# A recurrent transformer segment loop: left output products in one segment of a group, or by halves in two

## The chip, the cores and the metric

The kernel runs on one core of a Trainium2 chip. The core has TensorE (PE) for matrix products, VectorE (DVE), ScalarE (ACT) and GpSimd (POOL) for work on elements, SyncE (SP), which here only issues transfers, and 16 DMA engines. SBUF is the on-chip memory of 128 partitions; PE writes its results to PSUM, whose eight banks each hold 512 float32 values per partition. The metric is the device time of one execution in microseconds (us); the time before is the median of three executions.

## What is computed

```python
xn = layernorm(x)                                  # 2048 tokens x 1024
# A: 64 segments of 32 tokens, one after the other
mem = mem0                                         # 8 rows x 1024
for s in range(64):
    h = concat([mem, xn[32 * s:32 * s + 32]])      # 40 rows
    q, k, v = h @ Wq, h @ Wk, h @ Wv               # 32 heads of 128
    p = softmax(where(mask, q @ k.T * 128 ** -0.5, -1e9))
    o = (p @ v) @ Wo                               # 40 rows x 1024
    mem = o[:8]                                    # goes into the next segment
    outs.append(o[8:])
# B: a feed-forward block over all tokens
ff = gelu(xn @ w1 + b1) @ w2 + b2                  # inner width 3584
out = x + concat(outs) + ff
```

The four weight matrices of A hold 32 MB in bf16, and every segment needs all of them, so the segments' weights don't fit on chip. The memory rows make the segments a chain.

## The kernel before

**Stages.** First comes B with the layer norm, to about 440 us; its result plus x lies in DRAM as `R_n`. Then 64 segments run.

**Weights.** Each segment uses 64 weight tiles, called units, of 128 x 2048 (512 KB): 16 each of Q, K, V and O. 47 stay in SBUF. 17 are streamed, of which two are kept in PSUM and copied by DVE (L267) and 15 come by DMA on SP's queue (L278) through a ring of six slots; a slot is given the next streamed unit when PE is done with the one in it (`unit_done`). The order of the units is fixed by `PLACED`.

**Main and left rows.** A PE product with 32 columns of weights-side operand holds 32 rows of h, but a segment has 40. So the kernel takes 32 rows as "main": the first 24 of the segment's own rows (`NX`) and the 8 memory rows. The last 8 rows (`NL`) of four segments are put together into 32 "left" rows of a group (`GRP`), whose q, k and v are made for four segments at once. A segment's place in its group is `i4` = s mod 4. The left rows' products for K, Q and V are spread over the segments (`left_k`, `left_q`, `left_v`), one half (`u`, 16 heads) at a time. Left rows do not feed the memory, so they may be finished later.

**A segment.** `half_pass` makes K, Q and V of each half, `product` with four column tiles of 32 (L769, 512 columns each). Between them stand `scores` (L886, L892), `exps`, `sums` (L924, L930) and `values` (L978, L984), whose results are copied from PSUM by ACT for r = 0 and by DVE for r = 1 (L997). Then come the 16 O units (`O_UNITS`) with `o_product` (L1027); the value products of half 1 stand after unit `VALUES_1` = 5 among them.

**Output products.** In a segment without left output the main rows' products fill the four column tiles so: units 0 to 8 (`NPAIR` = 9) in products of 512 columns, two for each head; then `fold` adds the two halves of the bank together (ACT L1045, DVE L1048) while units 9 to 15 run in products of 256 columns into a new bank; a DVE add (L1163) makes the result. In the segment with left output (`left_o`: i4 = 1, and the last segment) every head has four products of 512 columns, two for the main rows and two for the 32 left rows of four segments, all into one bank `psX`, with no folding. ACT copies the bank (L1159). The memory rows of the result go through `put_mem` (L314, L324) into the next segment's h. Six units of left products of a coming half pass (`lead_products`) are made ahead to fill PE meanwhile.

**Results and small transfers.** The result is added to the segment's rows of `res_d` (L1184; loaded at L1124). A segment without left output stores its 24 rows straight to `out` (L1218, four stores). The one with left output adds its left rows to `resL_d` (loaded into `pd_main` at L1150), writes main and left rows to a DRAM buffer `outL_d` (L1190), and these are later copied DRAM to DRAM to `out` (L1215). Such copies, and the last of the copies from `R_n` into `res_d` and `resL_d` made by `turn_R` (L486), wait in a list `small`, from which `unit_done` issues one or two on POOL's queue. The loads and stores of segments 0 to 4 (`EARLY_SEGS` = 5) are issued by ScalarE, of later ones by GpSimd (`loads`).

**PSUM.** Three banks, `acc0` to `acc2`, are handed out by `new_acc` and given back by `let_go`; one bank, `mixed`, serves the scores, sums and memory rows; four, `kept`, hold the two weight units.

Of the kernel before, what the change touches and what calls it, by code (L numbers as in the profile page):

```python
# [17 lines left out]
P = 128  # L18
# [19 lines left out]
NX = 24  # L38
# [13 lines left out]
EARLY_SEGS = 5  # L52
# [12 lines left out]
AT_BANKS = 4  # L65

# [48 lines left out]
def kernel(  # L115
# [39 lines left out]
    outL_d = dram.tile([NGRP, 2 * SEG, DM], BF16, name="outL_d")  # L155
# [145 lines left out]
    left_outs, left_keys = [t[:, :, 0:SEG] for t in ko], [t[:, :, 2 * NL:] for t in ko]  # L301
# [29 lines left out]
    with tc.tile_pool(name="ma", bufs=2) as ma, tc.tile_pool(name="mps", bufs=6, space=PSUM) as mps:  # L331
# [95 lines left out]
        def keep_xT(tg, xnT):  # L427
            xl = [t[:, 0:512].rearrange("p (g k i t) -> p g k i t", g=2, k=KT, i=GRP) for t in ko_flat]
            for half in range(2):
                nc.sync.dma_start(  # L430
                    out=rows_d[16 * tg:16 * tg + 16, :, 128 * half:128 * half + 128].rearrange("s p c -> p s c"),
                    in_=xnT[half].rearrange("p s k t -> p s (k t)"),
                )
                for g in range(4):
                    nc.gpsimd.tensor_copy(
                        out=xl[g // 2][:, g % 2, 4 * half:4 * half + 4, :, :],
                        in_=xnT[half][:, 4 * g:4 * g + 4, :, NX:SEG].rearrange("p i k t -> p k i t"),
                    )
# [10 lines left out]
        def main_row(slot):  # L449

            return NL * slot + NL

        def with_left(seg):

            return seg % GRP == 1 or seg == NSEG - 1

        def turn_R(ttg, eng, small=None):

            for i in range(4):
# [3 lines left out]
                both = [  # L465
                    t.rearrange("(h r) c -> r h c", h=2)
                    for t in (res_d[min(4 * og + 1, NSEG - 1) + 1, :, :], resL_d[og, :, :])
                ]
                halves = [rows.rearrange("t (h w) c -> t w h c", w=2)[:, w, :, :] for w in range(2)]
                if with_left(seg):  # L470
                    m0 = SEG
                    pairs = [(both[w][m0:m0 + SEG, :, :], halves[w]) for w in range(2)]
                else:
                    pairs = [(res_d[seg + 1, :, :].rearrange("(j t) c -> t j c", j=4), rows)]
                rows_at = [NL * slot]
                if seg < 2:
                    rows_at.append(NL * (slot ^ 2))
                elif seg >= NSEG - 2:
                    rows_at.append(2 * NL + NL * slot)
                for r0 in rows_at:  # L480
                    pairs += [(both[w][r0:r0 + NL, :, :], halves[w][NX:SEG, :, :]) for w in range(2)]
# [192 lines left out]
    with tc.tile_pool(name="late", bufs=1) as late, \  # L674
# [67 lines left out]
        for s in range(NSEG):  # L742
# [15 lines left out]
            left_o = i4 == 1 or final  # L758
            og, slot = divmod(s + 2, GRP)
            m0 = SEG if left_o else main_row(slot)  # L760
# [80 lines left out]
            def turn_kL(ps, u):  # L841
                kL[u] = left_keys[u]
                turn(ps, kL[u], nc.vector.tensor_copy if first else nc.scalar.copy)
# [14 lines left out]
            def q_left(u):  # L858

                if i4 >= 2 + u and more:  # L860
                    q = qS[:, i4 - 2 - u, :, :]
                else:
                    q = qL[u][:, :, NL * i4:NL * i4 + NL]
# [6 lines left out]
            def keep_q(u):  # L870

                n = 2 - u
                copy_bits(
                    mixed[:, 340:340 + 64 * n].bitcast(U32).rearrange("p (i h t) -> p h i t", i=n, h=16),
                    qL[u].bitcast(U32)[:, :, (GRP - n) * NL // 2:].rearrange("p h (i t) -> p h i t", i=n),
# [22 lines left out]
            def exps(u):  # L898

                if u:  # L900
                    prA = q_all[:, 512:672].rearrange("p (c q) -> p c q", q=40)
                    c0 = 24 if i4 == 1 else 16
                    prB = ko[1][:, 0:8, c0:c0 + NL].rearrange("p (c a) q -> p c a q", a=2)
# [8 lines left out]
                for p, m in (  # L912
                    (prA[:, :, NL:SEG], mask_order), (prB, mask_left[:, i4, :].rearrange("p (a q) -> p a q", a=2))
# [5 lines left out]
            def sums(u):  # L919
# [25 lines left out]
                else:  # L945
                    c0 = 0 if first else NL * slot
                    pdB = left_outs[1 if first or i4 >= 2 else 0][:, :, c0:c0 + NL].rearrange(
# [22 lines left out]
            def values(u, rs):  # L970

                V, (pdA, pdB) = st["V", u], st["pd", u]
                av = {r: new_acc() for r in rs}
                oV = {r: av[r][:, 0:320].rearrange("p (c b q) -> p c b q", c=4, b=2) for r in rs}
                for c in range(4):
                    for r in rs:
# [3 lines left out]
                            start=(c == 0), stop=False, skip_group_check=True, tile_position=(64 * r, 0),  # L980
# [8 lines left out]
                for r in rs:  # L989
# [3 lines left out]
                        (left_outs[u][:, h, NL * slot:NL * slot + NL], 0, NL),  # L993
# [4 lines left out]
                    let_go(av[r])  # L998
# [9 lines left out]
            def o_product(n, t, acc):  # L1008
# [4 lines left out]
                for k in range(2):  # L1013
                    h = 4 * (i % 4) + 2 * u + k
                    main = (outM if i >= 4 else nat_home)[:, h, :]
                    if left_o:
                        lhs = [(0, 32, left_outs[i // 4][:, h, :]), (32, 32, main)]
                        tiles = [(64 * r + r0, w, (2 * r, 2 * r + 1), lhsT) for r0, w, lhsT in lhs for r in range(2)]
                        start, stop = n == 0 and k == 0, n == 15 and k == 1
                    elif n < NPAIR:  # L1020
                        tiles = [(64 * k + 32 * r, 32, (r, r + 2), main) for r in range(2)]
                        start, stop = n == 0, n == NPAIR - 1
                    else:
                        tiles = [(32 * r, 32, (r,), main) for r in range(4)]
                        start, stop = n == NPAIR and k == 0, n == 15 and k == 1
                    for r0, rows, blocks, lhsT in tiles:
                        nc.tensor.matmul(  # L1027
                            acc[r0:r0 + rows, 0:256 * len(blocks)],
                            lhsT=lhsT,
# [5 lines left out]
                        )  # L1035

# [82 lines left out]
            if apart:  # L1119
                ahead_v = left_keys[1]  # L1120
# [14 lines left out]
            at = {VALUES_1[i4]: [lambda: values(1, (0, 1))]}  # L1135
            if apart:
                at[VALUES_1[i4] + 1] = [moved_values]
            psX = new_acc()
            for n, unit in enumerate(O_UNITS):
                t = unit_tile(unit)  # L1140
                if n == NPAIR and not left_o:
# [6 lines left out]
                if n == 6 and left_o:  # L1148
                    st["resL"] = pd_main[:, 0:256]
                    loads.dma_start(  # L1150
                        out=st["resL"], in_=resL_d[og, :, :]
                    )
            nw = 2 if left_o else 1
            if not final:
                o_sb = outM
                no = 16 if left_o else 8
                o = psX[:, 0:32 * no].rearrange("p (h e) -> p h e", e=32)
                if left_o:
                    nc.scalar.copy(out=o_sb[:, 0:no, :], in_=o)  # L1159
                else:  # L1160
                    o = psX[:, 0:256].rearrange("p (h e) -> p h e", e=16)
                    flat = o_sb.rearrange("p h e -> p (h e)")[:, 0:256].rearrange("p (h e) -> p h e", e=16)
                    nc.vector.tensor_tensor(out=flat, in0=o, in1=st["folded"], op=ALU.add)  # L1163
                ahead = []
                if (i4 == 3 or more) and not final:
# [7 lines left out]
                put_mem(o_sb, nxt["hT"], mixed[:, 224:288], 4 // nw)  # L1173
# [3 lines left out]
            tiles = (res, st["resL"]) if left_o else (res,)  # L1177
            for w, r in reversed(list(enumerate(tiles))):
                if left_o:
                    o = psX[:, 256 * w:256 * w + 256].rearrange("p (h e) -> p h e", e=32)  # L1180
                else:
                    o = o_sb[:, 0:8, :]
                r_rows = r.rearrange("p (h e) -> p h e", e=32)
                nc.vector.tensor_tensor(out=r_rows, in0=o, in1=r_rows, op=ALU.add)  # L1184
                if left_o and not final:

                    for b in range(2):
                        c0 = 256 * (2 * b + w)
# [67 lines left out]
```

## Time and profile before

| what | us |
|---|---|
| time, median of three executions | 1810.41 |
| the three executions | 1801.45, 1810.41, 1812.01 |
| the profiled execution | 1811.68 |
| its span from the first to the last instruction | 1809.9 |
| groups 2 to 14, mean of one group of four segments | 85.4 |
| output stage of one segment with left output, first product to last, segments 8 to 61 | 7.5 to 8.6 |
| the same without left output | 4.5 to 6.8 |

The clock granted to PE was 0.998 of full speed. A group's time is taken from the starts of its output stages in the trace; the stages' times contain PE's waits in them. In the lines of the profile, PE is a matrix product and PEld the load of its weights-side operand, which is an instruction of its own and runs beside the products. In the first part, B, PE is full and the DMA engines are mostly idle; in the segments both are busy.

### The profile page before, as it was taken

What the parts mean: (1) busy time and instruction counts of PE and PEld (TensorE: products, weight loads), DVE (VectorE), ACT (ScalarE), POOL (GpSimd) and SP (SyncE); (2) the same over time, 40 slices, a digit from 0 to 9 for tenths busy, and PEclk for the clock granted to TensorE, in tenths of its full rate; (3) what the DMA queues carried; (4) which work ended last, traced back from release to release, by engine and by line L of the source; (5) the groups of instructions that cost most, each with busy time, mean ns of one, the idle gap of its engine ahead of it and who ended that gap; (6) DMA issues with size and microseconds to landing.
All of it is one profiled execution on the core that took longest, in us unless ns stands there. A gap on an engine that the chain in (4) does not pass through costs nothing.

```text
span 1809.9 us, 71522 instructions
## 1 busy us (share of the span) xinstructions
PE 1707.1 (94%) x31173; PEld 893.0 (49%) x31173; DVE 978.1 (54%) x2508; ACT 687.9 (38%) x1700; POOL 305.2 (17%) x595
## 2 busy tenths in 40 slices
PE   8999999998988999999999999999999999999997
PEld 4444444444444545545444555554545454555544
DVE  7657483804554555555555555555555555555554
ACT  6334260702333334333333334343433333434333
POOL 0000000411122211111111212111111111111111
PEclk9999999999999999999999999999999999999999
DMA  9931111769999999999999999999999999999997
GB/s 290 308 100 48 52 48 36 246 225 345 385 371 346 389 377 384 387 377 393 380 373 374 383 395 394 368 398 379 393 385 376 382 370 369 398 393 384 391 396 294
DMA packets 220870, 592.07 MB, mean 327 GB/s; under 512 B 46283, under 2 KB 75995, under 8 KB 220556
## 3 DMA queue, kind: packets, MB, share of 16 engines
q1 hardware_dynamic: 197652, 567.08, 83.5%
q0 software_dynamic: 17184, 17.23, 2.9%
q8 instruction: 244, 4.00, 0.9%
q10 hardware_dynamic: 5720, 3.19, 0.6%
q14 instruction: 70, 0.57, 0.1%
HBM read 573.43 MB, written 28.90 MB: 333 GB/s over the span
## 4 chain that ended last, share of the span: by engine, by line
PE 72%; DMA 13%; issue 6%; ACT 4%; DVE 3%; POOL 1%; ACTq 0%; DVEq 0%; POOLq 0%; SPq 0%
PE acc L769 34%; PE acc L1027 12%; PE ps L497 11%; PE ps L618 8%; DMA u<-Wc_O 7%; DMA u<-Wc_V 3%; PE ps L651 2%; ACT mixed L938 2%; PE acc L978 1%; DMA u<-Wc_Q 1%; PE mixed L886 1%; DVE kq L853 1%; DVE pd_main L951 1%; POOL res_d L486 1%; ACT kq L848 1%
## 5 line engine op out<-in xcount | busy, mean ns | idle before, releaser
L769 PE MATMUL acc<-u,hr_home 128*32 128x512 bf16 x11520 | 760.8, 380 | 15.7 <-issue 6.0
L769 PEld LDWEIGHTS <-hr_home 128*32 128x32 bf16 x12288 | 348.0, 96 | 285.5 <-issue 33.8
L769 PE MATMUL acc<-u,hrL 128*32 128x512 bf16 x2880 | 254.5, 380 | 4.4 <-issue 2.4
L497 PE MATMUL ps<-u 128*128 128x512 bf16 (+1 forms) x920 | 194.4, 373 | 2.0 <-ACT u L417 2.0
L267 DVE TENSOR_SCALAR u<-kept 128x512 uint32<-128x512 uint32 x254 | 163.1, 684 | 51.7 <-PE acc L769 39.2
L821 ACT CAST d_oL<-acc 128x512 bf16<-128x512 f32 x143 | 82.0, 585 | 261.0 <-PE acc L769 254.2
L618 PE MATMUL ps<-u 128*128 128x512 bf16 x672 | 147.0, 379 | 0.0
L1027 PEld LDWEIGHTS <-kq 128*32 128x32 bf16 x3908 | 103.1, 96 | 79.0 <-issue 22.2
L1027 PE MATMUL acc<-u,d_oL 128*32 128x512 bf16 x1944 | 133.9, 381 | 8.5 <-DMA u<-Wc_O 4.7
L497 PEld LDWEIGHTS <-u 128*128 128x128 bf16 x920 | 89.8, 98 | 104.9 <-issue 2.4
L1027 PE MATMUL acc<-u,kq 128*32 128x256 bf16 (+1 forms) x2372 | 117.2, 313 | 16.0 <-DMA u<-Wc_O 13.4
L853 DVE STREAM_TRANSPOSE kq<-kq 128x512 bf16<-128x512 bf16 x128 | 91.0, 711 | 74.8 <-ACT kq L848 72.6
L951 DVE TENSOR_TENSOR pd_main<-kq,mixed 128x320 bf16<-128x320 bf16 x128 | 62.4, 487 | 127.3 <-ACT mixed L938 127.3
L848 ACT CAST kq<-acc 128x512 bf16<-128x512 f32 (+2 forms) x192 | 85.3, 444 | 114.7 <-PE acc L769 85.1
L1218 POOL DMA_DIRECT2D out_dram<-hr_home x172 | 87.2, 514 | 227.3 <-DVE hr_home L1184 226.8
L825 ACT CAST kq<-acc 128x512 bf16<-128x512 f32 x128 | 75.2, 587 | 111.2 <-PE mixed L892 109.9
L769 PEld LDWEIGHTS <-hrL 128*32 128x32 bf16 x3072 | 86.3, 96 | 58.1 <-issue 5.9
L916 DVE TENSOR_TENSOR kq<-kq,mixed 128x96 bf16<-128x96 bf16 (+1 forms) x256 | 38.1, 190 | 125.7 <-ACT kq L906 70.5
L618 PEld LDWEIGHTS <-u 128*128 128x128 bf16 x672 | 65.3, 98 | 77.4 <-DVE g_u L579 0.4
L571 ACT ACTIVATE g_xb<-ps,b1col 128x512 bf16<-128x512 f32 x112 | 76.8, 686 | 55.6 <-PE ps L497 54.7
L938 ACT ACTIVATE mixed<-mixed,small_consts 128x160 f32<-128x160 f32 x256 | 94.2, 368 | 8.4
L1027 PEld LDWEIGHTS <-d_oL 128*32 128x32 bf16 x2592 | 63.8, 96 | 63.8 <-issue 16.1
(132 smaller groups left out, 2015.4 us busy)
## 6 DMA issues: line engine op xcount, KB each, us to landing
u<-Wc_K SPq DMA_DIRECT2D x256, 512.0 KB
u<-Wc_V SPq DMA_DIRECT2D x256, 512.0 KB
u<-Wc_O SPq DMA_DIRECT2D x256, 512.0 KB
u<-Wc_Q SPq DMA_DIRECT2D x192, 512.0 KB
u<-in_B_w_dram SPq DMA_DIRECT2D x28, 512.0 KB
u<-in_A_Wq_dram SPq DMA_DIRECT2D x13, 512.0 KB
u<-in_A_Wv_dram SPq DMA_DIRECT2D x12, 512.0 KB
u<-in_A_Wk_dram SPq DMA_DIRECT2D x9, 512.0 KB
```

Of the source, the lines that this page charges most:

```text
L267: nc.vector.tensor_single_scalar(out=out, in_=in_, scalar=0, op=ALU.bitwise_or)
L497: nc.tensor.matmul(ps[:, SEG * s0:SEG * s1].rearrange("p (s t) -> p s t", t=SEG), lhsT=w1_sb[fb // 2][:, kt, (fb % 2) * P:(fb % 2 + 1) * P ...
L571: nc.scalar.activation(out=xb[:, :], in_=ps[:, :], func=ACT.Identity, bias=b1col[:, fb:fb + 1], scale=1.0)
L618: nc.tensor.matmul(ps[:, :], lhsT=gts[fc // 4][:, fc % 4, t * P:(t + 1) * P], rhs=w2_sb[fc // 2][:, fc % 2, cs], start=(fc == 0), stop=(fc ...
L769: nc.tensor.matmul(o, lhsT=lhs[:, i, :], rhs=m, start=(i == seq[0]), stop=(i == seq[-1]), tile_position=(0, 32 * j),)
L821: cp(out=out, in_=ps.rearrange("p (h e) -> p h e", e=32))
L848: nc.scalar.copy(out=q_home[:, h0:h1, NL:40], in_=ps[:, 32 * h0:32 * h1].rearrange("p (h e) -> p h e", e=32))
L853: nc.vector.transpose(out=home, in_=home)
L938: nc.scalar.activation(out=mixed[:, 160 * b:160 * b + 160], in_=mixed[:, 0:160], func=ACT.Exp, scale=-1.0, bias=off[:, b:b + 1],)
L951: nc.vector.tensor_tensor(out=pdA.rearrange("p c b q -> p b c q"), in0=prA[:, None, :, :].to_broadcast([P, 2, 4, 40]), in1=dd, op=ALU.mult,)
L1027: nc.tensor.matmul(acc[r0:r0 + rows, 0:256 * len(blocks)], lhsT=lhsT, skip_group_check=True, rhs=o_columns(t, k, blocks), start=start, sto ...
L1218: loads.dma_start(out=out_flat[rows, 256 * j:256 * j + 256], in_=res[32 * j:32 * j + NX, :])
```

## The change

- The left output products move from segment i4 = 1 to segments 1 and 2, each of which makes them for half the columns: of each of the four 256-column blocks of the output, columns 0 to 127 in segment 1 and 128 to 255 in segment 2 (`l0`, `l1`). They have four column tiles of 128 columns for each head, and a bank of their own, `psY`. The main rows are made in all segments as in one without left output, with folding. The last segment makes its left rows at full width, 256 columns.
- `psY` is taken with `psX` ahead of the 16 units, so the value products of half 1 for r = 1 use its columns 128 on.
- The left rows' places (`columns`, `OWN`, `i_left`) alternate between groups, since a group's left values must now live until segment 2.
- The 24 main rows of every segment go straight to `out` by four stores. `outL_d` holds left rows alone and is written by halves; `resL_d` is loaded by halves, one unit later. The copies from `outL_d` to `out` are put into `small` after segment 2.
- `turn_R` makes fewer copies, since `res_d` and `resL_d` have one layout for all segments; `keep_xT` cuts two of its four POOL copies in two.
- `EARLY_SEGS` goes from 5 to 7.

```diff
-EARLY_SEGS = 5
+EARLY_SEGS = 7
...
+OWN = ((2, 3, 4, 5), (2, 3, 0, 1))
...
-    outL_d = dram.tile([NGRP, 2 * SEG, DM], BF16, name="outL_d")
+    outL_d = dram.tile([NGRP, P, 256], BF16, name="outL_d")
...
+    def columns(u, n):
+
+        c0 = 2 * NL * (n % 2)
+        return ko[u][:, :, c0:c0 + SEG]
...
-                for g in range(4):
+                for g, i0, i1, n in ((0, 0, 0, 4), (1, 0, 2, 2), (1, 2, 0, 2), (2, 0, 0, 4), (3, 0, 2, 2), (3, 2, 0, 2)):
                     nc.gpsimd.tensor_copy(
...
-                if with_left(seg):
-                    m0 = SEG
-                    pairs = [(both[w][m0:m0 + SEG, :, :], halves[w]) for w in range(2)]
-                else:
-                    pairs = [(res_d[seg + 1, :, :].rearrange("(j t) c -> t j c", j=4), rows)]
...
-                for r0 in rows_at:
-                    pairs += [(both[w][r0:r0 + NL, :, :], halves[w][NX:SEG, :, :]) for w in range(2)]
+                pairs = [(res_d[seg + 1, :, :].rearrange("(j t) c -> t j c", j=4), rows)]
+                left = resL_d[og, :, :].rearrange("(j t) c -> t j c", j=4)
+                slot ^= 2 * (og % 2)
+                for sl in [slot] + ([slot ^ 2] if seg < 2 or seg >= NSEG - 2 else []):
+                    pairs.append((left[NL * sl:NL * sl + NL, :, :], rows[NX:SEG, :, :]))
...
-            left_o = i4 == 1 or final
-            og, slot = divmod(s + 2, GRP)
-            m0 = SEG if left_o else main_row(slot)
+            left_o = i4 in (1, 2) or final
+            lg = NGRP if final else g
+            l0, l1 = (0, 256) if final else (128 * i4 - 128, 128 * i4)
+            o0 = NL * OWN[g % 2][i4]
+            i_left = i4 ^ (2 * (g % 2))
...
-                av = {r: new_acc() for r in rs}
+                shared = [st["psY"]] if u and left_o and not final else []
+                av = {r: shared[0][:, 128:] if shared and r else new_acc() for r in rs}
...
-                            start=(c == 0), stop=False, skip_group_check=True, tile_position=(64 * r, 0),
+                            start=(c == 0 and not (shared and r)), stop=False, skip_group_check=True,
+                            tile_position=(64 * r, 0),
...
-                    if left_o:
-                        lhs = [(0, 32, left_outs[i // 4][:, h, :]), (32, 32, main)]
-                        tiles = [(64 * r + r0, w, (2 * r, 2 * r + 1), lhsT) for r0, w, lhsT in lhs for r in range(2)]
-                        start, stop = n == 0 and k == 0, n == 15 and k == 1
-                    elif n < NPAIR:
-                        tiles = [(64 * k + 32 * r, 32, (r, r + 2), main) for r in range(2)]
+                    if n < NPAIR:
+                        tiles = [(64 * k + 32 * r, (r, r + 2)) for r in range(2)]
...
+                if left_o:
+                    for k in range(2):
+                        h = 4 * (i % 4) + 2 * u + k
+                        for j in range(4):
+                            c0 = DM * k + 256 * j
+                            nc.tensor.matmul(
+                                st["psY"][32 * j:32 * j + 32, 0:l1 - l0],
+                                lhsT=columns(i // 4, lg)[:, h, :],
+                                skip_group_check=True,
+                                rhs=t[:, c0 + l0:c0 + l1],
+                                start=n == 0 and k == 0,
+                                stop=n == 15 and k == 1,
+                                tile_position=(0, 32 * j),
+                            )
...
+            if final:
+                at = {4: [lambda: values(1, (0,))], 6: [lambda: values(1, (1,))]}
...
             psX = new_acc()
+            if left_o:
+                st["psY"] = new_acc()
             for n, unit in enumerate(O_UNITS):
                 t = unit_tile(unit)
-                if n == NPAIR and not left_o:
+                if n == NPAIR:
                     st["folded"] = fold(psX)
                     psX = new_acc()
...
-                if n == 6 and left_o:
-                    st["resL"] = pd_main[:, 0:256]
-                    loads.dma_start(
-                        out=st["resL"], in_=resL_d[og, :, :]
-                    )
+                if n == 7 and left_o:
+                    resL = pd_main[:, 0:l1 - l0]
+                    loads.dma_start(out=resL, in_=resL_d[lg, :, l0:l1])
...
-                put_mem(o_sb, nxt["hT"], mixed[:, 224:288], 4 // nw)
+                put_mem(o_sb, nxt["hT"], mixed[:, 224:288])
...
+            nc.vector.tensor_tensor(out=r_rows, in0=o_sb[:, 0:8, :], in1=r_rows, op=ALU.add)
+            if left_o:
+                nc.vector.tensor_tensor(out=resL, in0=st["psY"][:, 0:l1 - l0], in1=resL, op=ALU.add)
+                let_go(st["psY"])
+            eng = [nc.sync, nc.scalar] if final else [loads] * 2
+            for j in range(4):
+                eng[j % 2].dma_start(out=out_flat[rows, 256 * j:256 * j + 256], in_=res[32 * j:32 * j + NX, :])
...
             elif left_o:
...
+                loads.dma_start(out=outL_d[lg, :, l0:l1], in_=resL)
+            if i4 == 2:
+                done = outL_d[lg, :, :].rearrange("(j t) c -> t j c", j=4)
+                for x in range(GRP):
+                    row = (4 * lg - 2 + (x + 2 * (lg % 2)) % 4) * SEG + NX
+                    if row >= 0:
+                        o = out_flat[row:row + NL, :].rearrange("t (j c) -> t j c", j=4)
+                        small.append(lambda o=o, r=done[NL * x:NL * x + NL, :, :]: nc.gpsimd.dma_start(out=o, in_=r))
```

## The prediction

> **What bounds the kernel now.** First the page: engines, slices, DMA queues, chain.
>
> ```profile
> PE 1707.1 (94%) x31173; PEld 893.0 (49%) x31173; DVE 978.1 (54%) x2508; ACT 687.9 (38%) x1700; POOL 305.2 (17%) x595
> ...
> DMA  9931111769999999999999999999999999999997
> ...
> q8 instruction: 244, 4.00, 0.9%
> ...
> PE 72%; DMA 13%; issue 6%; ACT 4%; DVE 3%; POOL 1%; ACTq 0%; DVEq 0%; POOLq 0%; SPq 0%
> ```
>
> From 440 us on (the 64 segments) TensorE and the 16 DMA engines are both full; the chain lies on PE, with 13% waiting for weights and 6% "issue", idle time that no other engine ends. A window table shows how close the two are (columns: stretch, length, then busy time of each engine with its instructions, clock, DMA share, GB/s).
>
> ```profile
> 1055.00:1068.00 13.00, 12.53 (x287) 7.01 (x286) 8.88 (x21) 4.61 (x12) 2.58 (x5) 1.00 1.03 401
> 1078.00:1091.00 13.00, 13.00 (x272) 6.87 (x265) 6.28 (x17) 4.28 (x10) 4.12 (x8) 1.00 1.00 368
> 1099.00:1112.00 13.00, 12.81 (x310) 7.38 (x306) 7.55 (x19) 4.30 (x10) 2.60 (x5) 1.00 1.03 405
> ```
>
> The middle stretch follows the output products of a left segment (number 1 of a group); the DMA moves 368 GB/s there, 403 elsewhere. Next, who ended PE's waits from 623 to 1796 us, that is 13.75 groups of 85 us (total us, times, longest):
>
> ```profile
> PE acc L1027 <- DMA u<-Wc_O: 12.0, 27, 1.1
> ...
> PE acc L769 <- issue: 9.3, 14, 1.3
> PE acc L1027 <- issue: 5.4, 13, 0.8
> ...
> PE mixed L886 <- issue: 3.7, 5, 1.4
> PE acc L984 <- issue: 3.2, 5, 1.6
> PE mixed L892 <- issue: 2.8, 4, 1.4
> PE acc L769 <- DMA u<-Wc_V: 2.2, 7, 0.7
> ```
>
> Transfers hold PE for 14.2 us (1.0 a group), "issue" for 25.8 with the 1.4 of L978 (1.9 a group). What is "issue"? Two waits from the timeline, and what ran between neighbouring ones, from windows:
>
> ```profile
> 1487.33 0.83 PE L769 MATMUL acc<-low,hr_home 128*32 128x512 bf16 x12 [1.05 <-issue]
> ...
> 1500.04 0.40 PE L769 MATMUL acc<-u,hr_home 128*32 128x512 bf16 x4 [1.18 <-issue]
> ```
> ```profile
> 1480.62:1487.33 6.71, 5.63 (x129) 3.02 (x129) 4.09 (x11) 2.02 (x6) 0.27 (x1) 1.00 0.98 369
> 1487.33:1500.04 12.71, 11.00 (x258) 5.72 (x258) 7.22 (x19) 4.61 (x12) 2.58 (x5) 1.00 0.97 368
> ```
>
> Between them lie 129+129 and 258+258 instructions with those on the edges: 256 and 512. Queue q8 moved 4.00 MB in 244 packets: 64 bytes for each of PE's 62,346 products and weight loads, 256 of them in a packet. In the instruction records all 48 unexplained gaps of over 0.12 us in this stretch fall on the same place of a 256-instruction block, 1.24 to 1.62 us after a q8 packet ended (one: 2.3). So PE waits for its own instructions. In the records a block's packet starts only after PE has crossed into the block before it, and ends 2.7 to 5.2 us after (5 to 95%, median 4.1); with 1.28 us to the first instruction, a block costs at least 5.3 us in the median, 3.9 in the best twentieth. The packet's start came 1.8 us after the crossing with under 1.5 weight transfers outstanding, 3.5 us with over 3.5. A block of ordinary products (8 instructions in 0.217 us) works 6.9 us and hides that; a block of denser ones does not.
>
> **The change, part by part.** Product rates first, from the timeline.
>
> ```profile
> 1071.73 0.24 PE L924 MATMUL mixed<-kq,small_consts 128*32 128x160 bf16 x4
> 1071.80 0.20 PE L930 MATMUL mixed<-kq,small_consts 128*32 128x64 bf16 x4
> ...
> 1077.81 1.90 PE L1027 MATMUL acc<-u,kq 128*32 128x512 bf16 x32
> ...
> 1119.44 1.05 PE L1027 MATMUL acc<-u,kq 128*32 128x256 bf16 x32
> ```
>
> Four column tiles run together: (1.90-0.38)/7 = 0.217 us per set of 512 columns, (1.05-0.27)/7 = 0.11 per 256. Four of 160 columns give way after 0.07, four of 64 after 0.03, so 128 columns cost about 0.057 (an estimate between those two).
>
> *Products.* Segment 1 of a group: 32 sets of 512 = 6.94 us become 9 of 512, 14 of 256 (3.49 us) and 32 of 128 (1.82): 5.31. Segment 2: 3.49 becomes 5.31. A group gains nothing: +0.19 us. But instructions: 128 and 92 products become 220 and 220, each with its weight load, +440 a group, 1.72 blocks: from 1,822 products or 14.2 blocks a group to 16.0.
>
> *Blocks.* A left output stage now runs 440 instructions in 5.31 us, 256 in 3.09. A block with a share x of these works 6.94-3.85x us. With 5.3 us per block a wholly dense one waits 2.2 us; laid at random over block borders, the run of 1.72 blocks waits 2.9 us a segment (a wholly dense block lies in 72 of 100 positions, 1.6; the partly dense ones give 1.3). With 4.4 us (1.28 + 1.05 for the packet + 2.1, for the 1.2 to 2 transfers outstanding at the end of today's left stage) it is 1.4, with 3.9 it is 0.75. I take the middle of 2.9 and 1.4, since those stages lie between full and thin queues: 2.1 a segment, +4.2 a group. Half of today's other 1.5 us of "issue" falls away where the queue thins, -0.7; the 0.4 in L1027 are contained in the new figure, -0.4.
>
> The Trainium skill, "Runtime: NRT & Kernel Launch", section Instruction fetch mechanics, has blocks of 256 instructions, fetched while the current one runs, and calls the crossing mostly hidden. By that the 4.2 would be near 0, which is the balanced rival below; the trace agrees on the blocks and disagrees on the hiding, with 25.8 us of waits.
>
> *The shared bank.* Value products of half 1 now go into columns 128 on of psY; DVE copies them out while the next left products want the same bank. In all segments these copies end 0.62 us after the last value product; without a wait the next left product could start 0.15 after. If it waits: 0.53 us in segment 1, which waits for nothing there today, 0.35 in segment 2, which waits 0.2 one unit later. Queued behind it on PE: the rest of the stage. Bounds 0 and 0.88 a group; inside a dense block it eats from the block's wait, so +0.2. The Trainium skill, "PSUM — Partial Sum Buffer", section Terms, forbids two engines on one bank and quadrant at once. By that the upper bound is real; no trace here shows either.
>
> *Weight waits.* The evening-out ends the 1.0 us in which PE waits for transfers, most of it in segment 2: -1.0.
>
> *Small transfers.* Per group: 12 output stores from hr_home become 16; one 48 KB copy and two POOL stores go; outL_d and resL_d move in 256-byte rows, twice. By packet times in the trace (512 B 28 ns, 1 KB 47, 2 KB 84, 3 KB 126, 4 KB 169) 20.6 us of engine time become 19 to 27, over 16 engines -0.1 to +0.4 us: +0.1. POOL's queue: the four left-row copies wait for outL_d to land (5 us), and the next rows' load queues behind; today's five do the same and leave 4 us to spare. Folding in segment 1 (ACT 0.75, DVE 0.85 us) is hidden by seven units of at least 0.33; uncovered it costs 1.6. resL_d's load, issued a unit later, may land 0.5 us late for DVE; K's transpose is 2 us off.
>
> *Segments 0 to 6.* Waits from 559 to 580 us:
>
> ```profile
> DVE pd_main L1184 <- DMA pd_main<-resL_d: 4.2, 1, 4.2
> ...
> PE acc L769 <- DVE hr_home L1184: 3.1, 1, 3.1
> ```
>
> In segment 5 resL_d's load comes late from POOL, whose queue still holds the row copies; DVE and then PE stand. On ScalarE's queue that goes: -3.1 us once (0 to -5). Stores there wait for DVE ahead of K's eviction, 1.5 us off, as in segments 1 to 4. turn_R's fewer copies (8 for four segments, not 13 or 14) shorten POOL's queue. keep_xT cuts its POOL copies into more pieces while the feed-forward part runs, where the page shows POOL idle, and the swapped slots change addresses alone: nothing. End: the last segment's left products take 32 sets of 256 columns, 3.5 us as before, and one more DVE add follows, +0.3.
>
> **Sum.** A group: 4.2-0.7-0.4+0.19+0.2-1.0+0.1 = +2.6; 16 groups +41.6; with -3.1 and +0.3: +38.8. The profiled execution took 1811.7 us (span 1809.9 and 1.8 around it), 1.3 over the median: 1849.
>
> **Rivals.** *Balanced* (0.22): slower PE thins the weight queue until a block takes 3.9 us. Then 1.5-0.7-0.4+0.19+0.2-1.0+0.1 = -0.1 a group: about 1806. For it: packet delay follows the queue; against: the DMA stays near full at any period under 86 us, and 16.0 blocks at 5.3 are 85 us even if none of them wastes time. *Faster* (0.12): the DMA alone sets the pace and regains the thin stretch: 13 us x (1-368/403) = 1.1 us a group, 18 in all, with -3.1 gives 1790. For it: DMA share 1.00 to 1.03; against: PE has 82 us of work and waits a group. It decides if a dense block waits under 0.5 us. *Late rows* (0.04): POOL uses up its 4 us and PE waits 1 to 2 us in segment 3: 1830 or more, on its own. *Forecast* (0.62). Should the split not even the stages out, the waits for weights stay and the forecast gains 16 us.
>
> **Numbers.** Low end: the balanced case with its small transfers at their best, 1804. High end: 5.3 us a block (+1.5 a group) and no relief elsewhere (+0.7): 1884. One per cent is what a measurement can tell here (1792.3 to 1828.5 is "same"). Slower 0.66, same 0.22, faster 0.12.
>
> **What would show it.** q8 at about 272 packets, 34,750 products (3,520 more, 92 in the last segment, put_mem's 32 fewer); more "issue" waits at L1027, 256 instructions apart; output stages of 7 to 8 us in segments 1 and 2; over 390 GB/s behind segment 1 and fewer waits for Wc_O; no wait at L1184 near 567 us. Wrong if "issue" stays under 2 us a group, or if L1027 waits for DVE L997 beyond 0.6 us.

## The result, and the profile after

The changed kernel takes 1982.44 us (median of four, 1973.23 to 1990.87), the kernel before 1811.21 in the same set of runs: ratio 1.0954, 95% interval 1.0898 to 1.1011. The direction was foretold, the size was not: +171 us where the prediction had +38.8 and a range that ended at 1884. The profiled execution took 1985.56 us, its span 1983.6, with a mean granted clock of 0.974 against 0.998 before.

First the page of the changed kernel: engines, the instruction queue, and the chain of waits (shares of the span by engine, then by line).

```profile
PE 1754.1 (88%) x34733; PEld 959.9 (48%) x34753; DVE 999.0 (50%) x2575; ACT 690.0 (35%) x1718; POOL 308.6 (16%) x609
...
q8 instruction: 272, 4.46, 0.9%
...
PE 55%; DMA 22%; issue 12%; DVE 5%; POOL 3%; ACT 2%; DVEq 0%; ACTq 0%; SPq 0%; POOLq 0%
```

The counts are those foretold (272 packets, some 34,750 products). (In the changed kernel L755 are the products of K, Q and V, L1012 the output products of the main rows and L1026 those of the left rows.) The chain is another one: PE has 55% of it in place of 72%, "issue" 12% in place of 6%, DMA 22% in place of 13%, and the list by line has a transfer that the list of before did not name: the store of left rows, outL_d<-pd_main, with 8% of the span, more than the output products of L1012 (7%). The waits of all engines from 660 to 1960 us say who stands behind it (total us, times, longest):

```profile
DVE pd_main L937 <- DMA outL_d<-pd_main: 85.6, 26, 6.2
...
POOL out_dram L1197 <- DMA outL_d<-pd_main: 79.0, 13, 6.7
...
ACT kq L834 <- DVE d_oL L949: 56.4, 38, 4.6
...
PE acc L755 <- ACT kq L834: 53.4, 25, 3.9
...
DVE hr_home L1174 <- DMA hr_home<-res_d: 47.1, 16, 4.3
```

Read downwards it is one chain. VectorE's first sums of the next segment (L937) write `pd_main` and must wait until the store has read it, 26 times in 13 groups, up to 6.2 us; ScalarE's copy of Q (L834) waits for VectorE, PE for the copy. The second and fifth lines are GpSimd's copies of the left rows and, behind them on its queue, the load of `res_d`, which then comes late. The timeline shows one such case in a segment 1 of a group (start, length, what it is, and in brackets the idle time before it and who ended it); GpSimd, then VectorE, ScalarE and PE:

```profile
1150.66 2.04 POOL L1180 DMA_DIRECT2D out_dram<-hr_home  x4 [6.90 <-DVE pd_main L1176]
1157.12 0.56 POOL L1190 DMA_DIRECT2D outL_d<-pd_main  x1 [4.42 <-DVE mixed L268]
```
```profile
1150.17 0.28 DVE L1176 TENSOR_TENSOR pd_main<-acc,pd_main 128x128 bf16<-128x128 f32 x1
...
1162.69 0.49 DVE L937 TENSOR_TENSOR pd_main<-kq,mixed 128x320 bf16<-128x320 bf16 x1 [5.36 <-DMA outL_d<-pd_main]
```
```profile
1163.47 0.32 ACT L834 CAST kq<-acc 128x192 bf16<-128x192 f32 x1 [4.58 <-DVE d_oL L949]
```
```profile
1163.84 0.40 PE L755 MATMUL acc<-u,hr_home 128*32 128x512 bf16 x4 [3.90 <-ACT kq L834]
```

The add (L1176) is done at 1150.45. The four output stores go out by 1152.7, 0.5 us each; the store of `pd_main` goes out only at 1157.12. (The bracket names a VectorE operation that ended about then; the add that the store needs was long done.) In the records that is 0.31 us after the first of the four landed (1156.81), and so it is in 27 of the 28 segments whose store GpSimd issues; in the other one the first had landed by then. It lands at 1162.57, VectorE starts 0.12 later, and PE has stood for 3.90 us. Before, ScalarE issued that store 0.03 us after the add, and L951 never waited for it.

At the same time the waits that were foretold came too. PE's waits in the same stretch:

```profile
PE acc L1012 <- issue: 36.5, 26, 3.1
...
PE acc L1026 <- issue: 11.4, 10, 2.1
PE acc L1026 <- DVE kq L985: 9.4, 27, 0.3
...
PE acc L1012 <- DMA u<-Wc_O: 0.9, 3, 0.4
```

Issue waits at the output products are 47.9 us where they were 5.4 (in 13.75 groups); the wait for the shared bank is there (L985 is VectorE's copy of the value products); the waits for O weights are nearly gone, 0.9 for 12.0, though those for V, Q and K weights rose, to 9.0 us from 2.8. A window table for the case above (stretch, length, busy time of PE, PEld, DVE, ACT and POOL with instructions, clock, DMA share, GB/s):

```profile
1160.00:1163.84 3.84, 0.00 (x0) 0.03 (x1) 0.96 (x5) 0.32 (x1) 0.00 (x0) 1.00 1.01 404
1163.84:1168.00 4.16, 3.81 (x80) 1.58 (x83) 2.85 (x7) 1.40 (x5) 0.00 (x0) 0.60 0.71 214
```

While PE stands the weights keep coming at 404 GB/s until the ring is full (SyncE, which issues them, waits for PE 9.8 us in all between 1155 and 1172); then PE starts again at a granted clock of 0.60 and the DMA falls to 214 GB/s. So neither of the two full resources of before is full now.

### The profile page after: what moved, and what is told of

The parts are those of the page before. It is cut to its first block, busy times and chain, and to the rows that moved or that the text cites. A ratio compares the mean times of both kernels' runs of the same rounds, so it can differ in the third digit from the quotient of the medians.

```text
span 1983.6 us, 78855 instructions
## 1 busy us (share of the span) xinstructions
PE 1754.1 (88%) x34733; PEld 959.9 (48%) x34753; DVE 999.0 (50%) x2575; ACT 690.0 (35%) x1718; POOL 308.6 (16%) x609
## 4 chain that ended last, share of the span: by engine, by line
PE 55%; DMA 22%; issue 12%; DVE 5%; POOL 3%; ACT 2%; DVEq 0%; ACTq 0%; SPq 0%; POOLq 0%
PE acc L755 21%; PE ps L481 10%; DMA outL_d<-pd_main 8%; PE acc L1012 7%; PE ps L602 7%; DMA u<-Wc_V 5%; DMA hr_home<-res_d 4%; PE acc L1026 3%; DMA u<-Wc_O 3%; PE ps L635 2%; POOL out_dram L1197 1%; POOL out_dram L1180 1%; PE acc L965 1%; DVE u L268 1%; DVE kq L839 1%
## 5 line engine op out<-in xcount | busy, mean ns | idle before, releaser
L755 PE MATMUL acc<-u,hr_home 128*32 128x512 bf16 x11520 | 788.2, 388 | 81.3 <-ACT kq L834 33.9
L755 PEld LDWEIGHTS <-hr_home 128*32 128x32 bf16 x12288 | 351.9, 97 | 382.3 <-issue 127.1
L755 PE MATMUL acc<-u,hrL 128*32 128x512 bf16 x2880 | 257.0, 386 | 21.8 <-ACT kq L834 19.4
L1180 POOL DMA_DIRECT2D out_dram<-hr_home x224 | 113.7, 514 | 343.2 <-DVE pd_main L1176 191.9
L937 DVE TENSOR_TENSOR pd_main<-kq,mixed 128x320 bf16<-128x320 bf16 x128 | 62.5, 488 | 200.6 <-ACT mixed L924 111.4
L834 ACT CAST kq<-acc 128x512 bf16<-128x512 f32 (+2 forms) x192 | 85.2, 445 | 213.5 <-PE acc L755 120.7
L1012 PE MATMUL acc<-u,kq 128*32 128x256 bf16 (+1 forms) x2304 | 115.5, 293 | 21.1 <-issue 18.0
L1012 PEld LDWEIGHTS <-kq 128*32 128x32 bf16 x3840 | 102.3, 99 | 64.3 <-issue 44.0
L1012 PE MATMUL acc<-u,d_oL 128*32 128x512 bf16 x1536 | 127.4, 389 | 4.0 <-issue 2.8
L755 PEld LDWEIGHTS <-hrL 128*32 128x32 bf16 x3072 | 88.7, 97 | 73.2 <-issue 26.8
L1026 PEld LDWEIGHTS <-d_oL 128*32 128x32 bf16 x2112 | 61.2, 99 | 56.5 <-issue 35.3
```

What stands on the lines that cost most here:

```text
L755: nc.tensor.matmul(o, lhsT=lhs[:, i, :], rhs=m, start=(i == seq[0]), stop=(i == seq[-1]), tile_position=(0, 32 * j),)
L834: nc.scalar.copy(out=q_home[:, h0:h1, NL:40], in_=ps[:, 32 * h0:32 * h1].rearrange("p (h e) -> p h e", e=32))
L1012: nc.tensor.matmul(acc[r0:r0 + 32, 0:256 * len(blocks)], lhsT=main, skip_group_check=True, rhs=o_columns(t, k, blocks), start=start, stop= ...
L1026: nc.tensor.matmul(st["psY"][32 * j:32 * j + 32, 0:l1 - l0], lhsT=columns(i // 4, lg)[:, h, :], skip_group_check=True, rhs=t[:, c0 + l0:c0 ...
L1180: eng[j % 2].dma_start(out=out_flat[rows, 256 * j:256 * j + 256], in_=res[32 * j:32 * j + NX, :])
```

## The experiments

Theory after the result: the loss has two parts, (1) the store of `outL_d` moved from ScalarE's queue to the end of GpSimd's, (2) more instruction blocks for PE. Rivals: the late `res_d` rows, the shared PSUM bank, and the split of the columns as such. In the runs below "before" is the kernel before run on the same chip in the same set.

**The store back on ScalarE's queue**, all else as changed.

```diff
-                loads.dma_start(out=outL_d[lg, :, l0:l1], in_=resL)
+                nc.scalar.dma_start(out=outL_d[lg, :, l0:l1], in_=resL)
```

> The changed kernel, with the store of the left rows from pd_main to outL_d issued by ScalarE instead of GpSimd. Theory A (pd_main is held by this store, which stands behind four stores on POOL's queue, so DVE L937 of the next segment waits, 85.6 us in 13 groups, and ACT and PE behind it; POOL's copies of the left rows wait for its landing and make the loads of res_d late): those waits go, 4.4 to 8 us a group, 1982 becomes 1860 to 1916. Theory B (PE's instruction blocks are the main cost): the waits for L937 turn into others, above 1950. Theory C (the rows' loads are late for a reason of their own on POOL's queue): only the 4.4 us of segments 2 and 3 go, about 1916, and DVE L1174 still waits for res_d.

Measured 1895.7 us (1889.3 to 1899.85), before 1816.75; ratio 1.0431 [1.0403, 1.0459]. One word of the program is worth 87 us by the medians, 95 by the two ratios (1.0954 less 1.0431): more than half of the loss. The waits of L937 for the store are gone altogether, and PE's waits have another face (660 to 1860 us):

```profile
PE acc L1026 <- issue: 36.3, 23, 2.2
PE acc L1012 <- issue: 29.4, 25, 2.1
PE acc L1026 <- DVE kq L985: 9.4, 27, 0.3
```

**The store still on GpSimd's queue, but ahead of the four output stores.**

```diff
+            if left_o and not final:
+                loads.dma_start(out=outL_d[lg, :, l0:l1], in_=resL)
             eng = [nc.sync, nc.scalar] if final else [loads] * 2
...
-                loads.dma_start(out=outL_d[lg, :, l0:l1], in_=resL)
```

> The changed kernel, with the store to outL_d still on GpSimd but ahead of the four stores of the main rows. Theory A: it starts some 6 us earlier and lands about 5.5 us after the DVE add, just ahead of L937's need: 1865 to 1930, waits of L937 under 1 us a segment. Theory B: above 1950. Theory C: about 1916 with L1174 still waiting for res_d.

Measured 1899.11 us (1894.0 to 1900.11); ratio 1.0447 [1.0422, 1.0472], the same as on ScalarE. So it is the place in the queue that costs, not the engine. GpSimd's timeline shows that the wait has only moved to the transfer that is now last of five, where only GpSimd's own next load of rows (L287) waits for it:

```profile
1115.94 0.55 POOL L1179 DMA_DIRECT2D outL_d<-pd_main  x1 [7.57 <-DVE pd_main L1176]
1116.50 1.54 POOL L1182 DMA_DIRECT2D out_dram<-hr_home  x3
1121.08 0.51 POOL L1182 DMA_DIRECT2D out_dram<-hr_home  x1 [3.04 <-DMA out_dram<-hr_home]
```

**Two of the four output stores on ScalarE**, the store of `outL_d` behind the other two.

```diff
-            eng = [nc.sync, nc.scalar] if final else [loads] * 2
+            eng = [nc.sync, nc.scalar] if final else [loads, nc.scalar]
```

> The changed kernel, with the second and the fourth of the four output stores of a segment on ScalarE's queue; the store of outL_d stays on GpSimd, now behind two stores there instead of four. If the wait of that store for the first landing comes from the number of transfers that GpSimd has outstanding: it starts within 1.5 us of VectorE's add, VectorE's sums no longer wait for it, and the run comes to 1888 to 1905, as with the store on ScalarE. If the store waits for the output stores for another reason (order, data): it still starts some 4 us late, and the time stays over 1950.

Measured 1902.86 us (1897.08 to 1911.48), before 1814.42; ratio 1.0499 [1.0457, 1.054]. The third transfer follows the second without a wait:

```profile
1117.30 1.03 POOL L1180 DMA_DIRECT2D out_dram<-hr_home  x2 [6.55 <-DVE pd_main L1176]
1118.39 0.56 POOL L1190 DMA_DIRECT2D outL_d<-pd_main  x1
```

It starts 1.29 us after the end of the add (1117.10). Behind four the store waited, behind two it does not, and with the order turned round it is the last of the five that waits: it is what stands outstanding on GpSimd's queue that holds it, not its own data. The number alone is not the rule. In the version called "not split" below, a copy of 16 KB starts at once behind the same four stores, of which the first lands at 681.03 us, and only the next copy waits, until 0.31 us after that landing:

```profile
675.81 2.02 POOL L1182 DMA_DIRECT2D out_dram<-hr_home  x4 [6.32 <-DVE hr_home L1176]
677.81 0.58 POOL L1199 DMA_DIRECT2D out_dram<-outL_d  x1
681.34 0.56 POOL L1199 DMA_DIRECT2D out_dram<-outL_d  x1 [2.95 <-issue]
```

The store that waited as the fifth has 32 KB in 128 rows, the copy 32 rows. What the limit is, these runs do not say.

**The kernel before with more products.** In segment 1 each output product of 512 columns is made as two of 256: the same columns, 128 products and 128 weight loads a group more, 2,048 in all.

```diff
+                    parts = [0, 1] if left_o and not final else [None]
+                    for part in parts:
...
+                                blocks, c1 = blocks[part:part + 1], 256
```

> The kernel before, with the output products of segment 1 of a group made in twice as many products of 256 columns instead of 512: the same columns, 128 more products and weight loads a group, one more block of 256 instructions. If blocks of instructions cost PE what the prediction says (a dense block works 3.5 us and takes 4.4 to 5.3): 1.7 to 3.5 us a group, 1836 to 1866, with more issue waits at the output line. If instructions are free beyond their columns: 0.1 us a group, 1811 to 1815.

Measured 1862.2 us (1850.0 to 1865.81), before 1816.75; ratio 1.0227 [1.0192, 1.0263]: +45.5 us for 16 more blocks of 256 instructions. The waits name the place (640 to 1840 us; L1033 is the output product there, with 5.4 us of issue before):

```profile
PE acc L1033 <- issue: 37.3, 28, 2.8
```

**The kernel before with seven early segments.**

```diff
-EARLY_SEGS = 5
+EARLY_SEGS = 7
```

> The kernel before, with EARLY_SEGS = 7 alone. The prediction's term: PE's wait of 3.1 us near 567 us goes, 1806 to 1811. Rival: ScalarE's stores hold up its evictions in segments 5 and 6 by as much, 1811 to 1814.

Measured 1810.55 us (1803.72 to 1816.71, twelve runs), before 1816.75; ratio 0.9974 [0.9954, 0.9994], or -4.7 us with an interval of 1 to 8. Of all versions run this is the fastest beside its own "before".

**No shared bank** (with the store on ScalarE). The value products of half 1 take a bank of `new_acc`, at units 5 and 7.

```diff
-                shared = [st["psY"]] if u and left_o and not final else []
+                shared = []
...
+            if left_o and not final:
+                at = {5: [lambda: values(1, (0,))], 7: [lambda: values(1, (1,))]}
```

> Undone besides the store's queue (which made 1896 of 1982 us): the value products of half 1 have a bank of their own again, two units later in the left stages, as the unsplit stages place them. Theory A (the wait for the shared bank, 0.51 us in segments 1 and 2 each, is on PE's path): up to 1.0 us a group less, 1878 to 1885, and the waits of the left products for the value copies are gone. Theory B (in a dense instruction block PE waits for its instructions anyway, and the bank's wait only stands ahead of that): 1892 to 1900, with more issue time at the left products.

Measured 1901.97 us (1894.61 to 1906.76), before 1812.83; ratio 1.0481 [1.0438, 1.0525]: no gain. But the edit does not take the wait away, it exchanges it. The left products wait no longer, and the main ones wait for the same copies instead, since `new_acc` has three banks and the next `psX` comes after them (640 to 1840 us):

```profile
PE acc L1026 <- issue: 24.6, 17, 2.4
PE acc L1012 <- issue: 22.1, 24, 2.1
PE acc L1012 <- DVE kq L985: 12.3, 23, 0.8
```

12.3 us in place of 9.4. What the bank's wait costs by itself stays unmeasured; a version with a bank more wasn't tried, as there is none.

**Not split** (no shared bank, store on ScalarE). All left output columns in segment 1, as products of 256.

```diff
-            left_o = i4 in (1, 2) or final
+            left_o = i4 == 1 or final
...
-            l0, l1 = (0, 256) if final else (128 * i4 - 128, 128 * i4)
+            l0, l1 = 0, 256
```

> As the run without the shared bank, but the left output products are again all in segment 1 of a group, 128 of 256 columns in place of 256 of 128 columns: 128 products and 128 weight loads a group fewer, 2,048 in all, everything else of the change kept. Block theory (about 20 ns per product, from the 45 us that 2,048 more products cost the kernel before): 41 to 45 us under that run, 1838 to 1856, issue waits about half. Rival (the split evens out the stages and pays by fewer weight waits): no faster than that run, up to 16 us slower. Rival (instructions cost nothing, the rest of the 80 us over the kernel before is late transfers): within 5 us of that run.

Measured 1844.57 us (1840.37 to 1846.82); ratio 1.0164 [1.0121, 1.0208]. Undoing the split saves 57 us, more than the 41 to 45 expected. Issue waits of PE at the output products fall from 46.7 to 20.6 us, and the waits for weights rise again (640 to 1840 us):

```profile
PE acc L1026 <- issue: 12.3, 15, 1.6
...
PE acc L1012 <- issue: 8.3, 15, 1.3
...
PE acc L1012 <- DMA u<-Wc_O: 8.1, 19, 1.0
```

**The loads and stores on ScalarE in all segments**, once in the version not split and once in the kernel before.

```diff
-            loads = nc.scalar if s < EARLY_SEGS else nc.gpsimd
+            loads = nc.scalar
```

> As the run with the products unsplit, and in all segments the rows' loads, resL_d's load and the output stores are issued by ScalarE instead of GpSimd. If late rows (18 us of DVE waits for res_d with the store of outL_d on ScalarE, against none before) are on PE's path: 8 to 18 us under the unsplit run, and no wait of DVE for res_d is left. If they are hidden: within 4 us. Rival: ScalarE's waits for DVE ahead of each store hold its evictions, PE then waits for K or Q copies: 10 us or more slower.

> The kernel before, with the same loads and stores on ScalarE in all segments; the stored left rows stay on GpSimd as they are. If GpSimd's queue costs the kernel before nothing but the 3 us at segment 5: 1804 to 1812 (that saving, as with seven early segments, and no more). If ScalarE's waits ahead of the stores hold its evictions: 1820 or more. A wait of PE for ScalarE's copies beyond 1 us a group would show the second.

Measured 1858.72 us (1852.2 to 1864.65; ratio 1.0246 [1.0203, 1.0288]) and 1820.06 us (1813.98 to 1827.02; 1.0033 [1.0008, 1.0057]): slower than with GpSimd by 14 us in the first, by 6 in the second, which should have gained the 4.7 of the early segments. The edit did not take the late rows away: VectorE's waits for `res_d` rose, from 2.4 us to 11.0 in the version not split and from 11.5 to 27.7 in the kernel before. So what late rows cost is not tested by these two runs; in the version not split there were few of them. Nor did the rival's mechanism show: in both PE waits at most 1.2 us at L755 or L769 for a copy by ScalarE. PE waits more for O weights instead, 14.9 us where the unsplit version had 8.1, and 17.5 where the kernel before had 12.0 in nearly as long a stretch:

```profile
PE acc L1012 <- DMA u<-Wc_O: 14.9, 28, 1.0
...
DVE hr_home L1176 <- DMA hr_home<-res_d: 11.0, 21, 1.3
```
```profile
DVE hr_home L1184 <- DMA hr_home<-res_d: 27.7, 26, 2.4
...
PE acc L1027 <- DMA u<-Wc_O: 17.5, 39, 1.1
```

Why the weights come later then is open.

**Fewer products in the kernel before**, with seven early segments: eleven, then twelve units in products of 512 columns.

```diff
-NPAIR = 9
+NPAIR = 11
```

> The kernel before with seven early segments (alone: -4.7 us) and, in the three unsplit segments of a group, eleven instead of nine of the sixteen units of the output projection as products of 512 columns: 8 products fewer a segment, 24 a group, 384 in all with as many weight loads, the same columns: 3 blocks of 256 instructions fewer. Theory (2.8 us per block, from four runs with 12 to 28 more): 8.4 us less, with the early segments 1798 to 1803. Rival (only the dense output stages of the split pay for their blocks, ordinary ones hide it): 1806 to 1810. Rival (the fold behind the eleventh unit has five units, 1.6 us at 0.33 us each, to hide 1.6 us of ScalarE and VectorE; it shows): 1812 or more.

> As the one with eleven units, with twelve: 12 products fewer a segment, 576 in all, 4.5 blocks. Theory with the fold hidden: 12.6 us less, with the early segments 1793 to 1799. With the fold's 1.6 us against four units, 1.3 us: 0.3 us shown in each of 48 segments, which takes 14 us back: 1806 to 1814.

Measured 1811.82 us (twelve runs, 1806.65 to 1817.81; ratio 0.9978 [0.9959, 0.9997]) and 1818.77 (1815.28 to 1824.2; 1.002 [1.0002, 1.0037]). The first is no faster than seven early segments alone. The fold now shows: PE's memory rows (L314) wait for the add behind it (L1163), first with eleven, then with twelve units, 620 to 1790 us, where it was 1.3 us with nine:

```profile
PE mixed L314 <- DVE kq L1163: 8.6, 25, 1.0
```
```profile
PE mixed L314 <- DVE kq L1163: 16.9, 35, 1.4
```

With eleven, issue falls by 0.46 us a group and these and VectorE's other waits rise by 0.41; with twelve, issue does not fall. So whether fewer blocks would pay in a stage that is not dense is not settled: the fold took the gain, if there was one.

## What the time is made of

All versions over the same 13 groups (segments 8 to 59), us per group. Period: from the starts of the output stages; PE busy and what ended PE's idle time: from the window and waits views. The last two columns count the stretches of granted clock 0.5 in the clock records after 560 us and give their sum.

| version | period | PE busy | issue | DVE | ACT | DMA | half-clock stretches | us |
|---|---|---|---|---|---|---|---|---|
| before | 85.40 | 80.70 | 1.88 | 1.02 | 0.35 | 1.12 | 2 | 6.5 |
| before, more products | 89.11 | 81.96 | 4.28 | 1.02 | 0.42 | 1.07 | 10 | 35.3 |
| not split | 87.83 | 81.93 | 2.99 | 1.52 | 0.02 | 1.03 | 1 | 2.3 |
| store on ScalarE | 90.63 | 82.21 | 5.88 | 1.58 | 0.00 | 0.67 | 10 | 32.8 |
| as changed | 97.16 | 83.56 | 3.76 | 4.76 | 4.11 | 0.69 | 24 | 94.2 |

From the last row to the one above it: DVE and ACT waits 7.3 us, busy 1.4, issue back by 2.1 (presumably because a block's fetch goes on while PE stands; not tested), 6.5 in all. From there to the first row, 5.2: issue 4.0, busy 1.5, DVE 0.6, less 0.45 of waits for weights and 0.35 of waits for ACT.

Blocks against time, from the q8 packets (244 before): 16 more cost 45.5 us; 12 more, in the version not split, 31.7; 28 more, in the versions with the store moved, 79.0 to 89.1 (1895.7, 1899.11, 1901.97 and 1902.86, each less its "before"). That is 2.6 to 3.2 us per block in six versions, of which the four with the store moved share most of their program. It is what a block costs where short products are added, with the small other edits in it. It is not the wait for instructions alone: by the table, PE's busy time makes 1.3 of the 3.7 us a group with more products, and 1.2 of the 2.4 in the version not split.

## Why the prediction was right or wrong

- **Small transfers, +0.1: the step that failed.** It read "POOL's queue: the four left-row copies wait for outL_d to land (5 us), and the next rows' load queues behind; today's five do the same and leave 4 us to spare". It asked what queues behind the copies and not who waits for the store. The store had been on ScalarE's queue (`nc.scalar if w`), the change puts it on `loads`, behind four others, and the tile that it reads is VectorE's next target. The trace of before held the price of a delay: from the end of the add in segment 1 to L951 there are 8.0 us (7.5 to 8.1), and a store of these rows takes 6.0 us from issue to landing on GpSimd's queue (the median in the changed kernel's list of transfers), so about 2 us were to spare. As changed the store starts 4.75 us after the add on average, 2.3 us too late, twice a group; L937 starts 10.8 us after the add in place of 8.4 with the store on ScalarE. In the 57 segments that use GpSimd's queue 28 stores stand at 2.4 us, 67 us; measured were 87, or 95 by ratios. The rest can lie in the late rows and in the halved clock behind the stops (24 such stretches against 10); the runs do not take these apart.
- **Blocks, +4.2 less 0.7 and 0.4.** The mechanism is right: adding products to the kernel before, without adding columns, costs 45.5 us at the output products, and the issue waits rise by 4.0 a group in the changed kernel with the store on ScalarE. In the records of this last run the waits at the output products again follow the end of a q8 packet by 1.2 to 1.6 us, as in the prediction. The size was short: the prediction had a net 3.1, since half of the other issue waits was to fall away, and did not count the granted clock (below). The Trainium skill, "Runtime: NRT & Kernel Launch", section Instruction fetch mechanics, calls the crossing into a block mostly hidden. Where the products are short it is not: the 1.75 blocks more in a group came with the 4.0 us of issue waits.
- **Products, +0.19.** Counts right. Busy time rose by 1.5, part of it the clock; in the version not split, with hardly any half-clock time, busy time still rises by 1.2, and the runs do not take that apart.
- **Shared bank, +0.2.** The wait is real: 0.51 us in segments 1 and 2 by the gaps in the instruction records of the changed kernel (the waits view, which counts a product as busy until its modelled end, has 0.3), where the prediction had upper bounds of 0.53 and 0.35. Its price is not settled.
- **Weight waits, -1.0.** -0.45. Evening out the output stages was to give the DMA its thin stretch back; the left stages took 8.8 and 8.3 us as changed, and 9.1 and 9.8 with the store on ScalarE, instead of 7 to 8, so the DMA now idles twice a group. The sign "over 390 GB/s behind segment 1" failed: 12 us behind that stage carry 321 GB/s on average as changed, 323 with the store on ScalarE, 347 before.
- **Segments 0 to 6, -3.1.** -4.7 with an interval of 1 to 8; the wait near 567 us is gone. In the kernel before, that wait was followed by a stretch of 3.4 us at half clock (from 569.8 us), at most 1.7 us more, which the prediction did not count; with seven early segments no such stretch is there.
- **Rivals.** *Balanced* and *Faster* fell: a dense block waits up to 2.2 us, not under 0.5. *Late rows* occurred, as a consequence of the late store (47.1 us of waits for `res_d`, against 18.1 with the store moved and 11.5 before); what they cost by themselves is open, since with the loads on ScalarE these waits rose.

Without the store the change is +5.2 a group and not +2.6: 1811.2 + 16 x 5.2 - 4.7 = 1890, just beyond the high end of 1884. So the range failed twice: by a wait that was not seen, and by taking relief for granted that the lengthened stages themselves used up.

## What to carry to other kernels

When a DMA moves to another queue, ask three things of it: what stands ahead of it there, who writes next into the tile that it reads, and how many us that writer has to spare today, from the end of the last write to the start of the next. Four output stores ahead and some 2 us to spare cost 5% here, and putting the one urgent store first (or on the other queue) took it back. Where PE works on short products at a rate that its instruction supply doesn't follow, count products and not columns: each block of 256 instructions added cost 2.6 to 3.2 us in this kernel, so splitting a product to even out stages has to win more than that.

## What the runs showed of the hardware

**A transfer on GpSimd's queue can wait for an earlier one to land.** With four output stores outstanding the 32 KB store started 0.31 us after the first had landed, 0.9 to 4.7 us after the fourth had been issued (27 segments); with two outstanding there was no wait. A 16 KB copy behind the same four did not wait, the copy after it did.

**A stop can be paid twice.** In the run with the store on ScalarE (stretch, length, busy time of the engines, clock, DMA share, GB/s):

```profile
1126.00:1129.64 3.64, 1.42 (x48) 0.73 (x38) 0.89 (x4) 0.52 (x3) 0.55 (x1) 1.00 1.03 401
1129.64:1133.00 3.36, 3.36 (x80) 2.53 (x84) 2.12 (x4) 0.74 (x2) 0.00 (x0) 0.52 0.70 213
```

PE stood for 1.88 us at the end of the first stretch, then had half its clock for 3.4 us. Nine of the ten half-clock stretches of that run after 560 us follow such a stop, of 1.6 to 2.3 us; in the version not split, whose issue waits end at 1.6 us, one such stretch is left and no stop lies ahead of it. The length of the stop alone does not decide: of the 16 stops of 1.85 us or more after 560 us in the run with the store on ScalarE, 8 were not followed by half clock. The starts of the half-clock stretches lie on one grid of 3413 ns, and in the grid's interval just ahead of the nine PE was busy for 27 to 43% of the time; in the intervals that full clock followed, for 40% or more. It fits that what counts is how long PE stands within one interval; between 40 and 43% both came. Ten stretches are 32.8 us, 26.3 more than before; at half speed they cost at most 13 us, 0.9 a group, of the 1.5 by which busy time rose.

The Trainium skill, "TensorE: Matmul & The Clock Gate", section Part 1: The HAM clock gate, has the clock halved after at least one idle window of about 3.4 us, and such windows of 3413 ns. The length agrees (3413 ns in the clock records); the condition does not: intervals in which PE was busy for 27 to 43% of the time were enough here.
